# A first inverse product on 64 rows of TensorE per l, summed over c, in place of one on 128 rows

## The chip, the cores and the metric

One Trainium2 chip, one of its cores. The metric is the device time of one execution in microseconds; the time shown for a kernel is the median of several runs. TensorE is called PE in the profile, VectorE DVE, ScalarE ACT, GpSimd POOL, and SyncE, which issues most transfers, SP.

## What is computed

A Fourier filter along the sequence, then two expert layers on the 24576 rows that come out of it:

```python
X = np.fft.rfft(x, axis=1)                       # x: (8, 3072, 256)
Yr = Xr @ w_r - Xi @ w_i + b_r
Yi = Xr @ w_i + Xi @ w_r + b_i
Yr = np.sign(Yr) * np.maximum(np.abs(Yr) - 0.01, 0.0)
Yi = np.sign(Yi) * np.maximum(np.abs(Yi) - 0.01, 0.0)
x  = np.fft.irfft(Yr + 1j * Yi, n=3072, axis=1).reshape(-1, 256)
h  = np.maximum(x @ w_in, 0.0)                   # w_in: (256, 2048)
x  = h * h @ w_out                               # w_out: (2048, 256)
...
```

What follows (a soft mixture of 8 experts with 4 slots each) is not touched by the change.

## The kernel before

The transform of length 3072 is two products with small matrices, 96 x 32, and so is its inverse. The first part of the kernel works on 96 units, 12 for each of the 8 sequences. A unit holds two of 24 frequency groups; l (0 or 1) says which of the two, and c (0 or 1) the real or the imaginary part. A unit u goes through these steps, in the loop over half steps h (U = h // 2) at the end of the listing:

- `a_mm`, `a_out`: the product with the 96-point matrix, on PE (tile psA), copied out by ACT and written to DRAM (ad). It runs ahead of the units, at two thirds of a step per half step.
- `load_b`, `b_mm`: the values of two units come back from DRAM (bt), and the product with the 32-point matrix bm gives psB.
- `b_hi`, `b_lo`, `b_sum`: psB is split into a high and a low part (Xh, Xl), and a third operand, real plus imaginary, is formed (Sf, Sh, Sl).
- `l_mm`: the linear layer, as three products of split operands: psL and psS. psL's 128 rows are (l, k), 64 rows for each l; its columns are (c, d).
- `l_move`: DVE adds the bias to psS (st), and adds st to psL. It does so in four pieces of 64 rows by 256 columns, since the result ub has rows (c, k) and columns (l, d): each piece goes to another half of the rows.
- `l_relu`, `l_soft`: the soft threshold, on ACT (ua) and DVE (ub).
- `c_mm`, `c_out`: the first inverse product. PE takes for each l the 128 rows (c, k) of ub against cm, two matmuls of 256 columns into one bank (psC); ACT copies the bank (sc), and SP writes it to DRAM (zd) in four transfers.

All eight PSUM banks belong to one pool (psP, tag "g"), of which psA, psB, psL, psS and psC take a bank each in turn. The order on each engine is the order of the calls; nothing else schedules. In the even half step of U come `b_mm(U)`, `l_mm(U-2)`, `l_soft(U-4)`, `b_lo(U-1)`, `c_out(U-5)`, the first stage and `l_relu(U-3)`; in the odd one `c_mm(U-4)`, `l_move(U-2)`, `b_hi(U)`, `b_sum(U-1)`, the first stage and, for every second U, `load_b(U+3)`. Beside it `decode` unpacks the weights of the expert layer (operations from line 374 on, on DVE, ACT and POOL). In the last units the second inverse product of the first sequence is made (`stage_d`, psY, yf, yl). The second part of the kernel, the expert layers, begins with the first matmul into psA of line 633.

```python
            nc.tensor.matmul(p[:, l], lhsT=cm[:, 2 * (u % NU) + l], rhs=ub[:, l], start=True, stop=True)
```

is the matmul of the first inverse product, in `c_mm`.

Of the kernel before, what the change touches and what calls it, by code (L numbers as in the profile page):

```python
# [10 lines left out]
F32 = mybir.dt.float32  # L11
# [4 lines left out]
ALU = mybir.AluOpType  # L16
AX = mybir.AxisListType
PSUM = bass.MemoryType.PSUM
# [5 lines left out]
N2 = 32  # L24
NP = 24
DM = 256
# [7 lines left out]
def shape_constants():  # L34

    n1 = np.arange(N1)
    n2 = np.arange(N2)
    k = np.arange(48)
    ang = 2 * np.pi * np.outer(n1, k) / N1
    f1 = np.zeros((N1, N1))
    f1[:, :48] = np.cos(ang)
    f1[:, 48] = np.cos(np.pi * n1)
    f1[:, 49:] = -np.sin(ang[:, 1:])
    bm = np.zeros((2, 2, N2, NP, 2, 2, N2))
    cm = np.zeros((2, 2, N2, NP, 2, 2, N2))  # L50
    for p in range(NP):
        for h in range(2):
            k1 = p + NP * h
            for k2 in range(N2):
                if k1 == 0 and k2 == 0:
                    bm[0, h, :, p, 0, h, 0] = 1.0
                    bm[0, h, :, p, 1, h, 0] = (-1.0) ** n2
                    cm[0, h, 0, p, 0, h, :] = 1.0
                    cm[1, h, 0, p, 0, h, :] = (-1.0) ** n2
                elif k1 == 0:  # L60
                    kk, cin = (96 * k2, 0) if k2 < 16 else (48 + 96 * (k2 - 16), 1)
                    ph = 2 * np.pi * ((n2 * kk) % SEQ) / SEQ
                    bm[cin, h, :, p, 0, h, k2] = np.cos(ph)
                    bm[cin, h, :, p, 1, h, k2] = -np.sin(ph)
                    cm[0, h, k2, p, cin, h, :] = 2 * np.cos(ph)
                    cm[1, h, k2, p, cin, h, :] = -2 * np.sin(ph)
                else:
                    kk = k1 + 96 * k2
                    s = 1.0 if k2 < 16 else -1.0
                    ph = 2 * np.pi * ((n2 * kk) % SEQ) / SEQ  # L70
                    bm[0, h, :, p, 0, h, k2] = np.cos(ph)
                    bm[1, h, :, p, 0, h, k2] = np.sin(ph)
                    bm[0, h, :, p, 1, h, k2] = -s * np.sin(ph)
                    bm[1, h, :, p, 1, h, k2] = s * np.cos(ph)
                    cm[0, h, k2, p, 0, h, :] = np.cos(ph)
                    cm[1, h, k2, p, 0, h, :] = -s * np.sin(ph)
                    cm[0, h, k2, p, 1, h, :] = np.sin(ph)
                    cm[1, h, k2, p, 1, h, :] = s * np.cos(ph)

    order = np.array([NC * t + c for c in range(NC) for t in range(TB)])  # L80
    cm = cm[..., order]
    dm = np.zeros((N1, 104))
    dm[0, :N1] = 1.0 / SEQ
    dm[48, :N1] = np.cos(np.pi * n1) / SEQ
    dm[1:48, :N1] = 2 * np.cos(ang[:, 1:]).T / SEQ
    dm[49:, :N1] = -2 * np.sin(ang[:, 1:]).T / SEQ
    j = np.arange(128)
    cst = np.zeros((128, 4, 128))
    cst[:, 0] = np.eye(128)
    same = (j[:, None] % 32) == (j[None, :] % 32)  # L90
    cst[:, 1] = same
    for g in range(2):
        cst[:, 2 + g] = same & ((j[:, None] % 32) // 4 == 4 * g + j[:, None] // 32)
    f = np.float32
    return {
        "c_f1": f1.astype(f),
        "c_bm": np.ascontiguousarray(bm.reshape(128, NP, 128).astype(f)),
        "c_cm": np.ascontiguousarray(cm.reshape(128, NP, 128).astype(f)),
        "c_dm": dm.astype(f),
        "c_st": cst.astype(f),  # L100
    }
# [3 lines left out]
def fft_moe_kernel(ctx, tc, x, w_r, w_i, b_r, b_i, moe_w_in, moe_w_out, moe2_phi, moe2_w1, moe2_w2,  # L105
                   c_f1, c_bm, c_cm, c_dm, c_st, out):
    nc = tc.nc
# [4 lines left out]
    NU = NP // 2  # L112
# [56 lines left out]
    cm = k1p.tile([128, NP, 128], F32, tag="cm", name="cm")  # L169
# [13 lines left out]
    wkb = wka = psP = None  # L183
    xt, xs, pa, bt, pb, xb, sp, pl, sh, pc, ad = {}, {}, {}, {}, {}, {}, {}, {}, {}, {}, {}
    cur = {}

    def pbank(name):
        return psP.tile([128, 512], F32, tag="g", name=name)
# [109 lines left out]
            mm3(s, h[:, dh], l[:, dh], lwh[0][:, dh], lwl[0][:, dh], dh == 0, dh == 1)  # L298
        pl[u] = (p, s)

    def l_move(u):

        p, q = pl.pop(u)
        ub = wkb.tile([128, 2, DM], F32, tag="ub", name=f"ub{u}", bufs=3)
        st = wkb.tile([128, 2, DM], F32, tag="st", name=f"st{u}", bufs=1)
        nc.vector.tensor_tensor(out=st, in0=q.unsqueeze(1).broadcast_to([128, 2, DM]), in1=bias[u % NU == 0],
                                op=ALU.add)
        for l in range(2):
            s = slice(64 * l, 64 * l + 64)
            for c in range(2):  # L310
                nc.vector.tensor_tensor(out=ub[64 * c:64 * c + 64, l], in0=p[s, c], in1=st[s, c], op=ALU.add)  # L311
        sh[u] = [ub]

    def l_relu(u):
# [6 lines left out]
        nc.vector.scalar_tensor_tensor(out=ub, in0=ub, scalar=LAM, in1=ua, op0=ALU.add, op1=ALU.min)  # L321

    def c_mm(u):
        ub = sh.pop(u)[0]
        p = pbank(f"psC{u}").rearrange("p (l d) -> p l d", l=2)
        for l in range(2):
            nc.tensor.matmul(p[:, l], lhsT=cm[:, 2 * (u % NU) + l], rhs=ub[:, l], start=True, stop=True)  # L327
        pc[u] = p

    def c_out(u):  # L330
        b, k = divmod(u, NU)
        t = wkb.tile([128, 2, DM], F32, tag="sc", name=f"sc{u}")
        nc.scalar.copy(t, pc.pop(u))
        z = zd[b].rearrange("r c t d -> r (c t) d")
        for ch in range(4):
            r = NP * ch + 2 * k
            nc.sync.dma_start(out=z[r:r + 2].rearrange("q n d -> n q d"), in_=t[N2 * ch:N2 * ch + N2])


    wide = moe_w_in.dtype != F32  # L340
# [125 lines left out]
    XB, XL = 4, NB * NC  # L466
    with tc.manual_schedule():
        psp = ExitStack()
        psP = psp.enter_context(tc.tile_pool(name="psP", bufs=8, space=PSUM))
        wkbx, wkax = ExitStack(), ExitStack()  # L470
        wkb = wkbx.enter_context(tc.tile_pool(name="wkb", bufs=2, side="right", reuse_waits="tile"))
        wka = wkax.enter_context(tc.tile_pool(name="wka", bufs=2, side="right", reuse_waits="tile"))
# [17 lines left out]
            load_x(c)  # L490
        nc.sync.dma_start(bm[:, :4], c_bm[:, :4])
        wr, wi, wn = (wkb.tile([128, 2, DM], F32, tag="ub", name=s, bufs=3) for s in ("wr", "wi", "wn"))
        wm = wkb.tile([128, 2, DM], F32, tag="sc", name="wm")

        def copy(j):
            return nc.scalar.copy if j % 2 else nc.vector.tensor_copy
# [37 lines left out]
        def at(u, *steps):  # L534
            if 0 <= u < NT:
                for g in steps:
                    g(u)

        for h in range(2 * NT + 12):
            U, o = divmod(h, 2)  # L540

            j = -1
            if (h < 8 or (h + 1) * 2 // 3 > h * 2 // 3) and aj < NB * NA + 1:
                j, aj = aj, aj + 1
            def first_stage():
                if NA <= j < NB * NA:
                    a_mm(j)
                    if j % 2:
                        load_x(j // 2 + XB)
                if j >= NA + 1:  # L550
                    a_out(j - 1, nc.scalar.copy)

            if o == 0:
                at(U, b_mm)
                at(U - 2, l_mm)
                at(U - 4, l_soft)
                at(U - 1, b_lo)
                at(U - 5, c_out)
                first_stage()
                at(U - 3, l_relu)  # L560
            else:
                at(U - 4, c_mm)
                at(U - 2, l_move)
                at(U, b_hi)
                at(U - 1, lambda u: b_sum(u, nc.gpsimd))
                first_stage()
                if U % 2 and U + 3 < NT:
                    load_b(U + 3)

            if h % 4 == 2 and h < 18:  # L570
                nc.sync.dma_start(bm[:, h + 6:h + 10], c_bm[:, h + 6:h + 10])
            if h % 4 == 1 and h < 24:
                nc.sync.dma_start(cm[:, h - 1:h + 3], c_cm[:, h - 1:h + 3])
            if h == 14:
                nc.sync.dma_start(ident, c_st[:, 0])
                nc.sync.dma_start(dmt, c_dm)
                nc.sync.dma_start(phi, moe2_phi.rearrange("(a p) n -> p a n", p=128))
                nc.vector.memset(acc, 0.0)
                nc.vector.memset(ss, 0.0)
                nc.vector.memset(nm[0], 3.0e38)  # L580
            if h == 16:
                weight_tiles()
            if h > 16:
                for _ in range(1 + (h % 6 == 0)):
                    next(dec_run, None)
            if U == NT - YL and o == 1:
                drain(dec_run)
                wkax.close()
                yp[0] = ypx.enter_context(tc.tile_pool(name="yp0", bufs=1, reuse_waits="tile"))
                load_z(0)  # L590
                ylead = stage_d(0, pbank)
            if ylead is not None and U > NT - YL + 1:
                next(ylead, None)
# [246 lines left out]
        nM, cw, st = (rt.tile([128, 1], F32, tag=t, name=t) for t in ("nM", "cw", "st"))  # L840
# [7 lines left out]
        for n in range(NSB * NW + 1):  # L848
            s, q = divmod(n, NW)
# [110 lines left out]
        p = bank_o("01", "p_m2")  # L960
# [173 lines left out]
```

## Time and profile before

| | us |
|---|---|
| median of 3 runs | 2882.76 |
| lowest and highest of them | 2878.36, 2883.17 |
| the profiled execution: its time | 2878.61 |
| the profiled execution: its span | 2876.8 |
| of the span: PE busy | 2806.6 (98%) |
| of the span: DVE busy | 2149.8 (75%) |
| of the span: ACT busy | 1685.9 (59%) |

The span runs from the first instruction to the last. PE's busy time is made of starts that were recorded and ends that are modelled, so matmuls that follow each other closely overlap in it: where the rows give a time from one start to the next, that is what a matmul costs in a stream. A matmul of float32 leaves two records, two passes over the same columns; one of float32r (the products of split operands) leaves one. The first part of the kernel, which holds the change, is the first 534 us.

### The profile page before, as it was taken

The page shows a single profiled execution, that of the slowest core. Times are in us where ns is not written, and L with a number is a line of the kernel's source. Part 1 is how long each engine was busy: PE and PEld are TensorE (multiplying, and loading weights), DVE is VectorE, ACT ScalarE, POOL GpSimd, SP SyncE. Part 2 cuts the span into 40 slices and gives each one's busy share as a digit, 9 for nine tenths or more (in the row PEclk, how much of TensorE's full clock was granted, in tenths as well). Part 3 has the DMA queues.
Part 4 walks back from the last instruction along what each step waited for, and adds up shares of the span by engine and source line. Part 5 has one row for each costly group of instructions (what it writes and reads, how often), then busy time and mean ns, then how long its engine had stood idle before and what let it go on. Part 6 is the DMA issues. An engine that isn't in the chain of part 4 may idle for free.

```text
span 2876.8 us, 46778 instructions
## 1 busy us (share of the span) xinstructions
PE 2806.6 (98%) x17543; PEld 2639.8 (92%) x17543; DVE 2149.8 (75%) x4458; ACT 1685.9 (59%) x3720; POOL 174.2 (6%) x236
## 2 busy tenths in 40 slices
PE   8999999899999999999999999999999999999995
PEld 5788889899999999999999999999999999999974
DVE  4899999777777777777777777777777777777764
ACT  3677775565555656565656565656565656565543
POOL 0344541000000000000000000000000000000000
PEclk9999999999999999999999999999999999999997
DMA  9888885200000000000000000000000000000169
GB/s 270 230 231 228 237 219 144 61 12 12 15 12 15 12 15 12 15 12 15 12 15 12 15 12 20 12 15 12 18 14 15 12 15 12 15 12 4 37 234 367
DMA packets 106389, 190.07 MB, mean 66 GB/s; under 512 B 14930, under 2 KB 75730, under 8 KB 103218
## 3 DMA queue, kind: packets, MB, share of 16 engines
q1 hardware_dynamic: 102946, 180.78, 21.9%
q10 hardware_dynamic: 3216, 6.29, 0.6%
q8 instruction: 138, 2.26, 0.3%
q14 instruction: 89, 0.73, 0.1%
HBM read 108.38 MB, written 78.64 MB: 65 GB/s over the span
## 4 chain that ended last, share of the span: by engine, by line
PE 90%; DVE 5%; DMA 3%; ACT 1%; issue 1%; SPq 1%; POOL 0%; DVEq 0%; ACTq 0%; POOLq 0%
PE psA L633 19%; PE psX L633 14%; PE psO L119 12%; PE psO L120 12%; PE psO L118 12%; PE psY L433 4%; PE psA L208 3%; PE psC L327 2%; PE psB L243 2%; PE px L714 1%; DVE ub L311 1%; PE psL L118 1%; PE psL L119 1%; PE psL L120 1%; DMA out_dram<-ob 1%; PE pz L730 1%
## 5 line engine op out<-in xcount | busy, mean ns | idle before, releaser
L119 PE MATMUL psO<-gl,wo 128*128 128x384 f32 x2048 | 687.4, 336 | 0.0
L120 PE MATMUL psO<-gh,wo 128*128 128x384 f32 x2048 | 684.7, 334 | 0.0
L118 PE MATMUL psO<-gh,wo 128*128 128x384 f32 x2048 | 684.6, 334 | 0.0
L673 DVE TENSOR_TENSOR gl<-g,gh 128x384 fp32r<-128x384 f32 x1024 | 557.1, 552 | 91.1 <-ACT gh L656 75.4
L119 PEld LDWEIGHTS psO<-gl,wo 128*128 128x128 f32 x2048 | 384.4, 188 | 7.3 <-DVE gl L673 7.3
L120 PEld LDWEIGHTS psO<-gh,wo 128*128 128x128 f32 x2048 | 384.5, 188 | 0.0
L118 PEld LDWEIGHTS psO<-gh,wo 128*128 128x128 f32 x2048 | 384.5, 188 | 0.0
L633 PE MATMUL psA<-yh,wia 128*128 128x384 f32 x1024 | 353.2, 345 | 12.6 <-ACT r L649 12.1
L633 PE MATMUL psA<-yh,wib 128*128 128x384 f32 x1024 | 348.1, 340 | 0.9 <-ACT V L639 0.8
L633 PE MATMUL psX<-yh,wia 128*128 128x384 f32 x1024 | 343.1, 335 | 0.0
L644 DVE TENSOR_TENSOR h<-psX,r 128x384 f32<-128x384 f32 x256 | 142.7, 557 | 249.5 <-PE psX L633 247.7
L649 ACT ACTIVATE r<-psA 128x384 f32<-128x384 f32 x256 | 126.1, 492 | 303.3 <-PE psA L633 262.4
L665 DVE SCALAR_TENSOR_TENSOR g<-h 128x384 f32<-128x384 f32 x512 | 281.8, 550 | 0.1
L639 ACT COPY r<-psA 128x384 f32<-128x384 f32 x256 | 123.3, 482 | 262.9 <-PE psA L633 262.9
L644 DVE TENSOR_TENSOR h<-psX,W 128x384 f32<-128x384 f32 x256 | 142.8, 558 | 178.5 <-ACT W L639 177.6
L656 ACT CAST gh<-g 128x384 fp32r<-128x384 f32 x512 | 263.0, 514 | 14.7 <-DVE g L665 11.9
L667 DVE TENSOR_TENSOR g<-r 128x384 f32<-128x384 f32 x512 | 260.3, 550 | 0.1
L639 ACT COPY W<-psA 128x384 f32<-128x384 f32 x256 | 123.3, 482 | 222.3 <-PE psA L633 220.7
L658 ACT ACTIVATE gh<-r 128x384 fp32r<-128x384 f32 x512 | 240.7, 518 | 8.1
L633 PEld LDWEIGHTS psA<-yh,wia 128*128 128x128 f32 x1024 | 192.7, 188 | 27.9 <-ACT r L649 16.9
L644 DVE TENSOR_TENSOR h<-psX,V 128x384 f32<-128x384 f32 x256 | 141.7, 554 | 76.0 <-PE psX L633 68.6
L633 PEld LDWEIGHTS psA<-yh,wib 128*128 128x128 f32 x1024 | 192.4, 188 | 2.1 <-ACT V L639 1.7
(214 smaller groups left out, 5339.6 us busy)
## 6 DMA issues: line engine op xcount, KB each, us to landing
bt<-ad SPq DMA_DIRECT2D x192, 128.0 KB, 4.5
zd<-sc SPq DMA_DIRECT2D x384, 64.0 KB, 2.8
zt<-zd SPq DMA_DIRECT2D x64, 384.0 KB, 3.5
xt<-in_x_dram SPq DMA_DIRECT2D x63, 384.0 KB, 4.3
ad<-sa SPq DMA_DIRECT2D x56, 384.0 KB, 4.2
out_dram<-ob SPq DMA_DIRECT2D x21, 1024.0 KB, 18.3
w<-in_moe_w_dram SPq DMA_DIRECT2D x5, 1024.0 KB, 12.3
raw<-in_moe_w_in_dram SPq DMA_DIRECT2D x16, 256.0 KB, 3.8
```

The source lines that it names most:

```text
L118: nc.tensor.matmul(o, lhsT=ah, rhs=bh, start=start, stop=False)
L119: nc.tensor.matmul(o, lhsT=ah, rhs=bl, start=False, stop=False)
L120: nc.tensor.matmul(o, lhsT=al, rhs=bh, start=False, stop=stop)
L633: nc.tensor.matmul(p, lhsT=w[:, k, l], rhs=r[:, j], start=start and n == 0, stop=n == 2, skip_group_check=True)
L639: nc.scalar.copy(t, self.a)
L644: nc.vector.tensor_tensor(out=h, in0=self.x, in1=t, op=ALU.add)
L649: nc.scalar.activation(out=t, in_=self.g[k].pop() if k in self.g else self.a, func=AF.Relu)
L656: nc.scalar.copy(h, self.g[k][0])
L658: nc.scalar.activation(out=h, in_=self.g[k][0], func=AF.Square)
L665: nc.vector.scalar_tensor_tensor(out=g, in0=t, scalar=0.0, in1=t, op0=ALU.max, op1=ALU.mult)
L667: nc.vector.tensor_tensor(out=g, in0=t, in1=t, op=ALU.mult)
L673: nc.vector.tensor_tensor(out=l, in0=g, in1=f(h), op=ALU.subtract)
```

## The change

In `c_mm` the product is made for each l on that l's own 64 rows, (k) alone, and the two parts c are summed in PSUM by two matmuls, the first with `start`, the second with `stop`. The matmuls of l = 0 read rows 0 to 63 of ub and cm, those of l = 1 rows 64 to 127, and l = 0 and l = 1 write different banks. So ub stays in psL's layout, rows (l, k) and columns (c, d), and DVE's four moves become one addition (`l_add`). Two units share the two banks: the even unit takes the first half of the columns of each, the odd one the second. `c_out` copies both banks after the odd unit, and writes two units with four transfers. The pool psP gives 6 banks to tag "g" and 2 to tag "c". The constant cm is laid out anew to fit, sc is one buffer for two units where it was two buffers for one, and a start-up tile (wm) moves from sc's place to that of ua.

```diff
-        "c_cm": np.ascontiguousarray(cm.reshape(128, NP, 128).astype(f)),
+        "c_cm": np.ascontiguousarray(cm.reshape(2, 64, NP // 2, 2, 128).transpose(3, 1, 2, 0, 4).reshape(128, NP, 128)
+                                     .astype(f)),
...
-    def l_move(u):
+    def l_add(u):
...
-        for l in range(2):
-            s = slice(64 * l, 64 * l + 64)
-            for c in range(2):
-                nc.vector.tensor_tensor(out=ub[64 * c:64 * c + 64, l], in0=p[s, c], in1=st[s, c], op=ALU.add)
+        nc.vector.tensor_tensor(out=ub, in0=p, in1=st, op=ALU.add)
...
     def c_mm(u):
         ub = sh.pop(u)[0]
-        p = pbank(f"psC{u}").rearrange("p (l d) -> p l d", l=2)
-        for l in range(2):
-            nc.tensor.matmul(p[:, l], lhsT=cm[:, 2 * (u % NU) + l], rhs=ub[:, l], start=True, stop=True)
-        pc[u] = p
+        if u % 2 == 0:
+            pc[0] = [psP.tile([128, 2, DM], F32, tag="c", name=f"psC{u}_{l}", bufs=2) for l in range(2)]
+        for c in range(2):
+            for l in range(2):
+                s = slice(64 * l, 64 * l + 64)
+                nc.tensor.matmul(pc[0][l][:, u % 2], lhsT=cm[s, 2 * (u % NU) + c], rhs=ub[s, c], start=c == 0, stop=c == 1)
 
     def c_out(u):
-        b, k = divmod(u, NU)
-        t = wkb.tile([128, 2, DM], F32, tag="sc", name=f"sc{u}")
-        nc.scalar.copy(t, pc.pop(u))
+        if u % 2 == 0:
+            return
+        b, k = divmod(u - 1, NU)
+        t = wkb.tile([128, 2, 2, DM], F32, tag="sc", name=f"sc{u}", bufs=1)
+        for l in range(2):
+            nc.scalar.copy(t[:, :, l], pc[0][l])
+        t = t.rearrange("p u l d -> p (u l) d")
...
-            nc.sync.dma_start(out=z[r:r + 2].rearrange("q n d -> n q d"), in_=t[N2 * ch:N2 * ch + N2])
+            nc.sync.dma_start(out=z[r:r + 4].rearrange("q n d -> n q d"), in_=t[N2 * ch:N2 * ch + N2])
...
-        psP = psp.enter_context(tc.tile_pool(name="psP", bufs=8, space=PSUM))
+        psP = psp.enter_context(tc.tile_pool(name="psP", bufs=6, space=PSUM))
```

On PE, in the middle of the first part (the number behind a tile's letters is the unit's), the first inverse product of unit 56 stood between the linear layer of unit 58 and the next product of the first stage:

```order
L119 MATMUL psS58_4676<-lwl0_90,Sh58_4642 128x256
L120 MATMUL psS58_4676<-lwh0_87,Sl58_4643 128x256
L327 MATMUL psC56_4699<-ub56_4558,cm_86 128x256 x2
L208 MATMUL psA103_4717<-xt51_4267,f1t_84 96x512
L243 MATMUL psB61_4726<-bm_85,bt60_4494 128x2x64 x4
```

Now it stands at the same place, as four matmuls that go to two banks by turns:

```order
L120 MATMUL psS58_4473<-lwl0_90,Sh58_4439 128x256
L121 MATMUL psS58_4473<-lwh0_87,Sl58_4440 128x256
L329 MATMUL psC56_0_4497<-ub56_4366,cm_86 128x256
L329 MATMUL psC56_1_4498<-ub56_4366,cm_86 128x256
L329 MATMUL psC56_0_4497<-ub56_4366,cm_86 128x256
L329 MATMUL psC56_1_4498<-ub56_4366,cm_86 128x256
L209 MATMUL psA103_4515<-xt51_4086,f1t_84 96x512
L244 MATMUL psB61_4524<-bm_85,bt60_4298 128x2x64 x4
```

So every unit has, in one place, matmuls on 64 rows between matmuls on 96 or 128 rows; nothing else on PE has moved.

On ACT, a few units earlier, each unit had its copy of psC (unit 53, then unit 54) between others:

```order
L333 COPY sc53_4540<-psC53_4470 128x512
L219 COPY sa98_4492<-psA99_4488 96x512
L316 ACTIVATE ua55_4550<-ub55_4473,nlam_95 128x512
...
L123 CAST Sh57_4569<-Sf57_4537 128x256
L333 COPY sc54_4605<-psC54_4555 128x512
L219 COPY sa100_4615<-psA100_4546 96x512
L316 ACTIVATE ua56_4617<-ub56_4558,nlam_95 128x512
```

Now two copies stand behind the odd unit, and none behind the even one:

```order
L337 COPY sc53_4344<-psC52_0_4216 128x2x256
L337 COPY sc53_4344<-psC52_1_4217 128x2x256
L220 COPY sa98_4296<-psA99_4292 96x512
L314 ACTIVATE ua55_4355<-ub55_4280,nlam_95 128x512
...
L124 CAST Sh57_4374<-Sf57_4341 128x256
L220 COPY sa100_4414<-psA100_4351 96x512
L314 ACTIVATE ua56_4416<-ub56_4366,nlam_95 128x512
```

The copies of units 52 and 53 stand together, in the place of unit 53's.

## Rows read from the trace of the kernel before

**Rows 1.** The page: busy time of each engine over the span.

```profile
PE 2806.6 (98%) x17543; PEld 2639.8 (92%) x17543; DVE 2149.8 (75%) x4458; ACT 1685.9 (59%) x3720; POOL 174.2 (6%) x236
```

**Rows 2.** Windows: stretch, length, busy us (x records) of PE PEld DVE ACT POOL, clock, DMA, GB/s.

```profile
0.00:96.00 96.00, 80.31 (x386) 55.13 (x387) 48.47 (x102) 38.22 (x78) 9.01 (x15) 0.97 0.93 263
96.00:216.00 120.00, 118.95 (x770) 99.34 (x769) 113.55 (x246) 84.27 (x196) 53.03 (x73) 1.00 0.86 228
216.00:336.00 120.00, 119.79 (x784) 100.22 (x783) 113.56 (x245) 83.81 (x195) 55.24 (x73) 1.00 0.87 232
336.00:481.00 145.00, 145.00 (x995) 126.29 (x995) 133.34 (x287) 97.07 (x217) 49.50 (x66) 1.00 0.75 201
481.00:534.00 53.00, 44.47 (x316) 40.37 (x314) 50.63 (x103) 27.26 (x59) 7.40 (x10) 1.00 0.38 90
```

**Rows 3.** Chain of waits, 153 to 453 us: start, us, what.

```profile
153.33 0.86 PE psC L327 x4
154.20 0.86 PE psA L208 x2
155.06 0.89 PE psB L243 x8
...
159.77 0.89 PE psB L243 x8
...
449.46 0.89 PE psB L243 x8
...
453.31 0.89 PE psB L243 x8
```

**Rows 4.** Chain of waits, 480 to 540 us.

```profile
491.60 0.70 DVE ub L321
...
528.89 0.70 DVE ub L321
...
532.09 0.70 DVE ub L321
...
534.32 2.08 PE psC L327 x4
```

**Rows 5.** Chain of waits, 60 to 100 us.

```profile
72.88 4.96 DMA cm<-in_c_cm_dram
...
84.89 4.81 DMA raw<-in_moe_w_in_dram
```

**Rows 6.** Groups by line, 0 to 560 us: xcount | busy us, mean ns | idle before.

```profile
L311 DVE TENSOR_TENSOR ub<-psL,st 64x256 f32<-64x256 f32 x384 | 162.0, 422 | 7.1
L260 DVE TENSOR_TENSOR Xl<-psB,Xh 128x512 fp32r<-128x512 f32 x96 | 66.4, 691 | 3.1
L333 ACT COPY sc<-psC 128x512 f32<-128x512 f32 x96 | 56.3, 586 | 15.8 <-PE psC L327 15.0 <-DMA bt<-ad 0.3 <-DMA zd<-sc 0.3
```

**Rows 7.** Timeline at 2817.5 us: matmuls on 32 rows each, four row groups.

```profile
2817.33 0.76 PE L1093 MATMUL pf<-ro,cc 32*128 32x256 f32 x8
```

**Rows 8.** The tile pf: engine, count, duration ns min/median/max, first and last start.

```profile
L1093 PE MATMUL pf<-ro,cc x384: 374/375/792, 2810.8 to 2851.4; 32*128 32x256 f32 x192
```

**Rows 9.** Timeline of PE at 2739.5 us: start, us; 64*128 is 64 rows.

```profile
2739.69 0.33 PE L119 MATMUL psO<-gl,wo 128*128 128x384 f32 x1
2739.86 0.34 PE L120 MATMUL psO<-gh,wo 128*128 128x384 f32 x1
2740.13 0.40 PE L724 MATMUL py<-ident,lg 64*128 64x64 f32 x3
2740.37 0.35 PE L724 MATMUL py<-ident,e 64*128 64x64 f32 x3
2740.65 0.45 PE L633 MATMUL psA<-yh,wia 128*128 128x384 f32 x1
```

**Rows 10.** Timeline of PE at 1528 us, from 32 columns back to 128.

```profile
1527.72 0.83 PE L706 MATMUL pl<-xm,phi 128*32 128x384 f32 x8
1528.48 0.44 PE L633 MATMUL psA<-yh,wia 128*128 128x384 f32 x1
```

**Rows 11.** Windows, psC alone: stretch, length, busy us (x records) PE PEld ACT, clock, DMA, GB/s.

```profile
96.00:216.00 120.00, 25.20 (x96) 17.60 (x95) 13.41 (x23) 1.00 0.86 228
216.00:336.00 120.00, 23.86 (x92) 16.69 (x92) 14.08 (x24) 1.00 0.87 232
336.00:481.00 145.00, 30.98 (x120) 21.44 (x120) 17.17 (x30) 1.00 0.75 201
```

**Rows 12.** Waits of PE and its weight loads, 96 to 481 us: total, times, longest.

```profile
PEld psC L327 <- DVE Sf L261: 2.1, 8, 0.3
PEld psC L327 <- DVE ub L321: 2.1, 4, 1.1
...
PE psC L327 <- DVE ub L321: 1.3, 3, 0.8
PEld psC L327 <- DVE Xl L260: 1.1, 4, 0.3
```

More of the change, by code (lines that the diff above doesn't have):

```diff
@@ L324, in c_mm, with c_out @@
         ub = sh.pop(u)[0]
-        p = pbank(f"psC{u}").rearrange("p (l d) -> p l d", l=2)
-        for l in range(2):
-            nc.tensor.matmul(p[:, l], lhsT=cm[:, 2 * (u % NU) + l], rhs=ub[:, l], start=True, stop=True)
-        pc[u] = p
-    def c_out(u):
-        b, k = divmod(u, NU)
-        t = wkb.tile([128, 2, DM], F32, tag="sc", name=f"sc{u}")
-        nc.scalar.copy(t, pc.pop(u))
+        if u % 2 == 0:
[4 more added lines that the diff above has]
+                nc.tensor.matmul(pc[0][l][:, u % 2], lhsT=cm[s, 2 * (u % NU) + c], rhs=ub[s, c], start=c == 0, stop=c == 1)
+    def c_out(u):
+        if u % 2 == 0:
+            return
+        b, k = divmod(u - 1, NU)
+        t = wkb.tile([128, 2, 2, DM], F32, tag="sc", name=f"sc{u}", bufs=1)
+        for l in range(2):
+            nc.scalar.copy(t[:, :, l], pc[0][l])
+        t = t.rearrange("p u l d -> p (u l) d")
         z = zd[b].rearrange("r c t d -> r (c t) d")
@@ L492, in fft_moe_kernel @@
         wr, wi, wn = (wkb.tile([128, 2, DM], F32, tag="ub", name=s, bufs=3) for s in ("wr", "wi", "wn"))
-        wm = wkb.tile([128, 2, DM], F32, tag="sc", name="wm")
+        wm = wkb.tile([128, 2, DM], F32, tag="ua", name="wm", bufs=1)
         def copy(j):
@@ L562, in fft_moe_kernel @@
                 at(U - 4, c_mm)
-                at(U - 2, l_move)
+                at(U - 2, l_add)
                 at(U, b_hi)
```

## The prediction

> **What bounds the kernel now.** I read first the busy times of the span, then windows by stage, then the chain of waits in the stage that the change touches, then the groups of instructions, and last the few places where PE already does what the change asks of it.
>
> PE is busy 98% of the span and DVE 75% [rows 1]. An average says little, so the windows: from 96 to 481 us PE is busy 118.95 of 120, 119.79 of 120 and 145.00 of 145 us, DVE 113.55, 113.56 and 133.34 [rows 2]. Both look full. Which of them sets the pace is told by the chain: there it consists of PE's matmuls without a gap, psC 0.86, psA 0.86, psB 0.89 us, and two units are 159.77 - 155.06 = 4.71 us apart [rows 3]. **PE is the bound of this stage**; DVE is just fast enough. Late in it, where psA has run out, a unit takes PE 453.31 - 449.46 = 3.85 us [rows 3].
>
> From 481 to 534 us it is the other way round: DVE is busy 50.63 of 53 us, PE 44.47 [rows 2], and the chain runs from one soft threshold to the next, eight of them in 528.89 - 491.60 = 37.29 us, 4.66 each [rows 4]. **DVE is the bound there.** The first 96 us wait for transfers: PE is busy 80.31, and the chain has two waits of nearly 5 us for DMA, cm and raw [rows 2, 5].
>
> **The change part by part.**
>
> *DVE.* Four additions of 64x256, 422 ns each, go: 1.69 us a unit. One of 128x512 comes; its nearest row is the subtraction from psB in the same shape, also PSUM with SBUF, 691 ns [rows 6]. So 1.0 us less for every unit.
>
> *PE, the matmuls themselves.* Before: four records of 256 columns in 0.86 us, 0.215 each [rows 3]. After: eight, each of 256 columns, on half the rows. Whether the halves run beside each other is shown where the output is made: there matmuls of 32 rows and 256 columns float32 go to four row groups and four banks, and eight records take 0.76 us from the first start to the last end [rows 7]; one after the other they would need 7 x 0.215 = 1.5 us before the last began, and one lasts 0.37 [rows 8]. So row groups do overlap. Two groups then make four steps of 0.215 out of eight records: 0.86 again, **nothing gained or lost**. The other extreme, no overlap, is eight steps, 1.72 us.
>
> *PE, going into the tile of 64 rows and out.* The kernel has this form once: six small matmuls on 64 rows between two on 128 [rows 9]. In a stream the psO matmuls start 0.17 us apart and last 0.34, so one starts 0.17 before its predecessor's modelled end (2739.69 and 2739.86). The first on 64 rows starts at 2740.13, only 0.07 before the end at 2740.20. PE's pipeline ran empty for 0.10 more. On the way back it is the same: the six end at 2740.37 + 0.35 = 2740.72, psA starts at 2740.65, 0.07 before. The way back from 32 columns gives 0.07 as well (1527.72 + 0.83 = 1528.55 against 1528.48) [rows 10]. So 0.10 each way. And the first matmul after a switch has its weights' load in front of it, which elsewhere lies under the matmul before: psA takes 0.45 us there instead of psO's 0.34 for the same 128x384, 0.11 more [rows 9]; going in, the first three take 0.40 and the next three 0.35, 0.05 more [rows 9]. I take 0.10 going in, since psC's weights are 128 columns wide like psA's. **Sum: 0.10 + 0.10 + 0.10 + 0.11 = 0.41 us a unit.** Bounds: 0.20 if both loads stay hidden, 0.65 if each way costs the whole overlap of 0.17 and each load 0.15.
>
> From 96 to 481 us psC has 96 + 92 + 120 = 308 records [rows 11], four to a unit: 77 units. PE is the bound, so 77 x 0.41 = **+31.6 us**. (Bounds +15.4 and +50.)
>
> *DVE's stalls of PE in that stage.* They go, since DVE gets 1.0 us of slack and PE is slower. PE is idle 1.05 + 0.21 + 0 us in the windows [rows 2]; the rows that name DVE before psC add up to 2.1 + 2.1 + 1.3 + 1.1 = 6.6 [rows 12], partly under matmuls still running. I take **-2** (bounds 0 and -6.6).
>
> *The last stage.* DVE needs 4.66 - 1.0 = 3.66 us a unit, PE 3.85 + 0.41 = 4.26. PE becomes the bound, 0.40 less than 4.66, for the 46 us from 483 to 529, ten units: -4.0. Behind them lies one more l_move before the last thresholds (529 to 532 us) [rows 4], -1.0; the last psC, 2.08 us [rows 4], is followed by psA and pays its own switch, some +0.4. Together **-4.6**.
>
> *The first 96 us.* Some six units' psC lie there. Their 2.5 us is put under the wait for raw, which ends when it lands; I take 0 (bounds 0 and +2.5).
>
> *ACT, SP and the banks.* ACT has the same two copies of 586 ns for two units [rows 6], and is busy 84 of 120 us [rows 2]. SP issues half as many writes for the same bytes. A pair of units now waits for both copies of the pair before it, since each bank of psC has no second buffer. But the copies stand one half step ahead, and between psC of the odd unit and the next pair's psC lie psB, twelve psL and six psS, about 4.71 - 0.86 - 0.86 = 3 us [rows 3], against 1.17 us of copies; I cost it at nothing. If ACT's queue were half a microsecond late, it would be paid once in two units, 38 x 0.5 = 19 us. With six banks psL and psS take banks that DVE freed in the unit before; DVE now frees them earlier than it did. Nothing.
>
> Sum: 31.6 - 2 - 4.6 + 0 = **+25 us**, on the profiled execution's 2878.61: 2903.6. The median of the runs lies 4.15 above that execution, so 2907 to 2908; I say 2907. Of a difference from no change about 0.2%, 5.8 us, can be told here.
>
> **The rivals.**
>
> *1. The switch is free, and only DVE's saving is left (faster).* Were the weights loaded and the pipeline kept full across the change of tile, PE would stay at its pace, DVE's stalls (-2) would go, and in the last stage the bound would fall from 4.66 to PE's 3.85, -8, and the tail -1: 2882.8 - 11 = 2872. It decides at a price of 0.08 us a unit, where 77 units cost the 6 us that the end gives back. For it: the rows show one switch to 64 rows, with small transposes. Against: three switches, two kinds of tile, the same 0.10 [rows 9, 10]. Chance 0.08.
>
> By the Trainium skill (TensorEngine Tiling (Array Packing), Key Properties) a change of tiling mode drains the engine; it gives no size, and by it alone this rival would have no chance. The 0.10 each way agrees.
>
> *2. The row groups do not run beside each other here.* Eight steps in place of four, 0.86 more for each of 77 units, +66: 2973. Against: [rows 7], though with 32 rows and without sums in a bank. Chance 0.05.
>
> *3. The second pass of a float32 matmul holds up the other row group.* If the two passes of l = 0 must start before the first of l = 1, the steps form a staircase: five instead of four, 0.215 x 77 = +17: 2924. Against: eight records in such a staircase need at least four steps, 3 x 0.215 + 0.37 = 1.02 us, and took 0.76 [rows 7]. Chance 0.04.
>
> The Trainium skill (TensorE: Matmul & The Clock Gate, Part 3, what overlaps and what doesn't) says that matmuls are strictly first in, first out, without reordering, which taken for passes gives this rival; the 0.76 us disagrees.
>
> *4. The banks.* The pair's wait of the last part, +19: 2926. Chance 0.03.
>
> **How the numbers follow.** Forecast 0.80, rivals as above. The forecast's own range: price 0.20 to 0.65 a unit, +15.4 - 9 = +6 to +50 - 5 = +45, most of it between 2889 and 2927; rivals 3 and 4 end within it. Rivals 1 and 2, 0.13 together, and some of the forecast's ends stay outside: 2888 to 2928. Faster by over 0.2%: rival 1 and a little, 0.09. The same: a price near 0.1, 0.05. Slower: the rest, 0.86.
>
> **What would show it.** In the profile after: eight psC records a unit that take about 1.07 us on the chain where four took 0.86, and a load of weights in the open behind them, before psA or psB, so that two units are 5.1 us apart where they were 4.71; DVE's group of 128x512 additions at about 690 ns x96, and DVE busy some 85 of 120 us where it was 113; in the last units psB 4.26 us apart, on PE; the first psA of line 633 near 560 instead of 536 us. I am wrong if psC's eight records are stretched over 1.5 us or more (rival 2), if psA or psB starts 0.215 behind the last psC (rival 1), or if PE waits for ACT's copy sc before an even unit's psC (rival 4).

## The result and the profile after

| | before | after |
|---|---|---|
| median, us | 2881.76 (four runs) | 2903.11 (four runs) |
| lowest and highest, us | 2878.36, 2883.17 | 2900.64, 2908.02 |
| profiled execution: time, span | 2878.61, 2876.8 | 2900.64, 2898.8 |

The ratio of after to before is 1.0078, interval 1.006 to 1.0095: **21 us slower**. The prediction said 2907, between 2888 and 2928. The profiled executions differ by 22.03 us; where these lie is told from them.

The page of after, busy time by engine ([rows 1]):

```profile
PE 2836.1 (98%) x17927; PEld 2632.5 (91%) x17927; DVE 2039.9 (70%) x4170; ACT 1691.3 (58%) x3720; POOL 177.5 (6%) x236
```

DVE has lost 110 us of work, PE has gained 30, and the time went with PE. By stage, the windows of after (the columns of [rows 2]):

```profile
96.00:216.00 120.00, 120.00 (x822) 91.91 (x822) 82.03 (x165) 82.36 (x187) 51.60 (x69) 1.00 0.81 222
216.00:336.00 120.00, 120.00 (x822) 92.06 (x820) 80.81 (x163) 80.97 (x182) 54.26 (x72) 1.00 0.77 213
336.00:481.00 145.00, 145.00 (x1003) 111.87 (x1000) 95.59 (x189) 93.74 (x208) 52.53 (x67) 1.00 0.75 203
481.00:534.00 53.00, 53.00 (x432) 47.39 (x433) 37.67 (x72) 31.08 (x66) 8.07 (x12) 1.00 0.44 118
```

From 96 to 534 us PE is never idle. DVE went from 113.55 to 82.03 of 120 us and waits: in the groups by line of after (0 to 580 us; line, engine, operation, count, busy us, mean ns, idle before and its cause; [rows 6]) the operation ahead of the addition, st, waits 141.3 us for psS, where it waited 14.3 us in before (last line, 0 to 560 us).

```profile
L309 DVE TENSOR_TENSOR ub<-psL,st 128x512 f32<-128x512 f32 x96 | 66.4, 691 | 3.3
L307 DVE TENSOR_TENSOR st<-psS,bias 128x512 f32<-128x512 f32 x96 | 66.3, 691 | 146.7 <-PE psS L121 141.3 <-DMA bias<-in_b_r_dram 5.4
```

```profile
L306 DVE TENSOR_TENSOR st<-psS,bias 128x512 f32<-128x512 f32 x96 | 65.7, 684 | 20.2 <-PE psS L120 14.3 <-DMA bias<-in_b_r_dram 5.6
```

The addition takes 691 ns x96, as the subtraction of the same shape did before. On PE, the chain of waits of after in the long stage ([rows 3]):

```profile
161.06 1.06 PE psC L329 x8
162.13 1.09 PE psB L244 x8
...
166.21 1.06 PE psC L329 x8
167.28 1.03 PE psA L209 x2
```

psC's eight records take 1.06 us where four took 0.86: +0.20. Whatever follows psC is longer too: psA 1.03 where it took 0.86, psB 1.09 where it took 0.89. Two units are 166.21 - 161.06 = 5.15 us apart. Call a stretch of matmuls on 64 rows, between matmuls on 96 or 128 rows, a visit to the 64-row tile. So **a visit to the 64-row tile costs 0.37 or 0.40 us**. The timeline of after shows it at one switch (start, us, engine, line, tile):

```profile
546.37 0.28 PE L120 MATMUL psS<-lwl,Sh 128*128 128x256 f32 x1
...
546.49 0.28 PE L121 MATMUL psS<-lwh,Sl 128*128 128x256 f32 x1
546.70 0.73 PEld L329 LDWEIGHTS psC<-ub,cm 64*128 64x128 f32 x8
546.70 1.14 PE L329 MATMUL psC<-ub,cm 64*128 64x256 f32 x8
...
547.76 0.19 PEld L119 LDWEIGHTS psL<-lwh,Xh 128*128 128x128 f32 x1 [0.33 <-issue]
547.76 0.39 PE L119 MATMUL psL<-lwh,Xh 128*128 128x256 f32 x1
...
547.99 0.28 PE L120 MATMUL psL<-lwl,Xh 128*128 128x256 f32 x1
```

The psS matmuls start 0.12 apart; psC starts 0.21 behind the last of them, 0.09 more. The loads of psC and psL begin together with their matmuls, not under the matmul before, and psL's first matmul takes 0.39 where the next takes 0.28.

In the last units ([rows 4]) the chain, which was DVE's, is PE's, with psC 4.23 us apart; then it goes to ACT and to transfers of sc:

```profile
505.28 1.06 PE psC L329 x8
...
509.51 1.06 PE psC L329 x8
...
543.38 1.06 PE psC L329 x8
...
546.77 1.06 PE psC L329 x8
...
550.15 1.11 PE psC L329 x8
...
553.65 2.29 DMA zd<-sc
...
558.45 2.40 DMA zd<-sc
...
...
562.02 1.33 PE psA L638 x3
```

**Where the 22.03 us lie**, from the starts of the same matmuls in both traces (each unit's first psL; the expert layers' first psA and first psO), beside the forecast's terms:

| from | to | the end's time in before | shift there in after | of it in this stretch | forecast |
|---|---|---|---|---|---|
| start | unit 9 | 98.1 | -0.7 | -0.7 | 0 |
| unit 9 | unit 86 (77 units) | 485.2 | +26.2 | +26.8 | +31.6 - 2 |
| unit 86 | first psA | 535.8 | +19.0 | -7.2 | -4.6 |
| first psA | first psO | 543.3 | +22.7 | +3.8 | 0 |
| first psO | end | 2876.8 | +22.0 | -0.7 | 0 |

### The profile page after: what moved, and what is told of

It reads as the page before. It is cut to its first block, busy times and chain, and to the rows that moved or that the text cites. A ratio compares the mean times of both kernels' runs of the same rounds, so it can differ in the third digit from the quotient of the medians.

```text
span 2898.8 us, 46941 instructions
## 1 busy us (share of the span) xinstructions
PE 2836.1 (98%) x17927; PEld 2632.5 (91%) x17927; DVE 2039.9 (70%) x4170; ACT 1691.3 (58%) x3720; POOL 177.5 (6%) x236
## 4 chain that ended last, share of the span: by engine, by line
PE 93%; DMA 3%; DVE 2%; SPq 1%; ACT 1%; issue 0%; POOL 0%; DVEq 0%; ACTq 0%
PE psA L638 18%; PE psX L638 14%; PE psO L120 12%; PE psO L121 12%; PE psO L119 12%; PE psY L438 4%; PE psA L209 4%; PE psC L329 3%; PE psB L244 3%; PE psL L119 2%; PE psL L120 2%; PE psL L121 2%; PE px L719 1%; DMA out_dram<-ob 1%; PE pz L735 1%; PE pl L711 1%
```

## The experiments

Theory A: PE bounds the first part, and the change pays a fixed price for each visit to the 64-row tile; the rest is the wait for the single sc buffer at the end. The rivals are named with each run.

### The addition alone

```diff
-        for l in range(2):
-            s = slice(64 * l, 64 * l + 64)
-            for c in range(2):
-                nc.vector.tensor_tensor(out=ub[64 * c:64 * c + 64, l], in0=p[s, c], in1=st[s, c], op=ALU.add)
+        nc.vector.tensor_tensor(out=ub, in0=p, in1=st, op=ALU.add)
```

This is the kernel before with that edit only; it leaves out the change on PE, so its product mixes l and c and is not the reference's.

> The kernel before, with DVE's part of the change alone: one addition of 128x512 in place of the four moves. ub is then left in the linear layer's rows while PE's two matmuls on 128 rows stay as they were, so the first inverse product mixes l and c. PE's work is that of the kernel before, to the instruction. Theory A (PE bounds the long stage; DVE's relief is worth its few stalls there and the last units): the stalls of about 3 us, the last units from 4.66 to 3.85 us each, about 8, and the tail 2 go: 13 us faster than before, about 2869. Theory B (DVE and PE bound the stage together, so 1.0 us a unit counts in full): 77 us faster, about 2805. If PE's steady pace is 4.71 and 5.57 us between units as before, A holds.

Measured: 2867.81, ratio to before 0.9951 (0.9938 to 0.9965), 14.3 us faster. Its chain in the long stage and in the last units:

```profile
159.28 0.86 PE psC L324 x4
...
163.98 0.86 PE psC L324 x4
...
168.74 0.86 PE psC L324 x4
...
502.48 0.86 PE psC L324 x4
...
506.33 0.86 PE psC L324 x4
```

163.98 - 159.28 = 4.70 and 168.74 - 163.98 = 4.76: the long stage keeps its pace with DVE relieved of 1 us a unit, so PE bounds it; the last units go from DVE's 4.66 to PE's 3.85. By the starts of the same matmuls, as in the table above, the 77 units of the long stage take 2.3 us less than in before, and the stretch from unit 86 to the first psA 10.8 less. That is what DVE's part of the change is worth when nothing is paid for it on PE.

### Half as many visits, and c = 0 and c = 1 apart

The first joins the matmuls of an even and an odd unit. The other two make c = 1 a visit of its own, behind the next unit's linear layer or ahead of it.

```diff
         if u % 2 == 0:
-            pc[0] = [psP.tile([128, 2, DM], F32, tag="c", name=f"psC{u}_{l}", bufs=2) for l in range(2)]
+            return
+        pc[0] = [psP.tile([128, 2, DM], F32, tag="c", name=f"psC{u}_{l}", bufs=2) for l in range(2)]
+        for v in (u - 1, u):
+            ub = sh.pop(v)[0]
...
```

> The changed kernel, with the matmuls on 64 rows of two units behind each other, after the odd unit: half as many visits to the tile of 64 rows, the same matmuls. Theory A (the loss is the way into the tile of 64 rows and back, about 0.38 us a visit): 38 visits fewer in the stage that PE bounds and some in the last units, 15 to 18 us less than the changed kernel, about 2887, still slower than before; two units 10.2 us apart become 9.85. Theory B (the eight matmuls themselves are slower on half the rows, or six banks hold PE up): the time of the changed kernel, 2903, or a little more, since DVE's addition now waits for a longer stretch of PE.

```diff
+    def c_half(u, c):
+        ub = sh[u][0]
+        for l in range(2):
+            s = slice(64 * l, 64 * l + 64)
+            nc.tensor.matmul(pc[0][l][:, u % 2], lhsT=cm[s, 2 * (u % NU) + c], rhs=ub[s, c], start=c == 0, stop=c == 1)
...
-                at(U - 5, c_out)
+                at(U - 5, lambda u: c_half(u, 1), c_out)
```

> The changed kernel, with each unit's four matmuls on 64 rows in two places: c = 0 where they stand, c = 1 in the half step after, behind the linear layer. Twice as many visits to the tile of 64 rows, the same matmuls. Theory A (the loss is about 0.38 us a visit): 77 visits more in the stage that PE bounds and 11 in the last units, 29 to 34 us more than the changed kernel, about 2935. Theory B (the matmuls themselves are slower, or the banks hold PE up): the time of the changed kernel, 2903, within 3 us.

```diff
                 at(U, b_mm)
+                at(U - 5, lambda u: c_half(u, 1))
                 at(U - 2, l_mm)
```

> The changed kernel, with c = 1 of each unit's matmuls on 64 rows moved to the next half step, behind psB and ahead of the linear layer: every unit goes into the tile of 64 rows twice, and ACT's copy sc, which held PE up where c = 1 stood behind the linear layer, has the linear layer's 2 us to itself again. Theory A (0.36 to 0.39 us a visit): 96 visits more, of which some 89 in stretches that PE bounds, 32 to 35 us more than the changed kernel, about 2937; each four records on 64 rows then take 0.32 + 0.215 us of PE, and psC in the chain two pieces a unit. Theory B (a visit costs more when it is short, as the 56 us of the run before suggests, 0.6 a visit): 2955 or more, without PE waiting for sc.

| | median, us | ratio to before | against after, us |
|---|---|---|---|
| two units joined | 2883.91 | 1.0007 (0.9998 to 1.0016) | -19.2 |
| c = 1 behind the linear layer | 2958.95 | 1.0268 (1.0254 to 1.0283) | +55.8 |
| c = 1 ahead of it | 2933.2 | 1.0185 (1.0171 to 1.0199) | +30.1 |

Chain of two units joined, then of c = 1 ahead of the linear layer:

```profile
162.40 0.86 PE psA L209 x2
163.26 1.93 PE psC L331 x16
165.19 1.03 PE psA L209 x2
```

```profile
159.36 0.63 PE psC L331 x4
160.00 1.03 PE psA L209 x2
```

One visit with 4, 8 or 16 records takes 0.63, 1.06 and 1.93 us. At two records to 0.215 us these would be 0.43, 0.86 and 1.72: each time 0.20 or 0.21 more, and psA behind it 0.17 more. **The price belongs to the visit and not to its length**, and both doubling and halving the visits moved the time accordingly, by 30.1 us for a forecast of 32 to 35 and by 19.2 for 15 to 18. The traces show it without the scatter of the runs: from unit 9 to unit 86 (77 units) the shift against before is +13.2 us with a visit for two units, +26.8 with one for each (after), +55.2 with two (c = 1 ahead of the linear layer). That is 13.7 us for 38.5 visits and 28.4 for 77, 0.36 and 0.37 each.

The middle run missed its 2935 by 24 us, and it tells little of the price. Its waits from 150 to 430 us (engine, line, waited for, us in total, times, longest) have two that the others lack:

```profile
PEld psC L331 <- ACT sc L341: 22.7, 32, 1.1
...
PE psC L331 <- ACT sc L341: 5.3, 8, 0.7
```

With c = 1 so late, ACT's copies came too late for the next pair's banks. That is the wait of rival 4, brought about by the experiment; besides, where no psA stands between c = 1 of one unit and c = 0 of the next, two visits run into one. The run ahead of the linear layer has neither.

### The buffer of sc

The last two pairs of units write sc into buffers of bt, which is no longer used there.

```diff
-        t = wkb.tile([128, 2, 2, DM], F32, tag="sc", name=f"sc{u}", bufs=1)
+        if u < NT - 3:
+            t = wkb.tile([128, 2, 2, DM], F32, tag="sc", name=f"sc{u}", bufs=1)
+        else:
+            t = wkb.tile([128, 4, DM], F32, tag="bt", name=f"sc{u}").rearrange("p (u l) d -> p u l d", u=2)
```

> The changed kernel, with the last two pairs of units copied into buffers of their own (bt's, which nothing loads any more) in place of the single sc. Theory A (at the end of the first part ACT waits for the write of the pair before, and the expert layer's first copies queue behind it): the waits of ACT before sc, some 5 us in the trace of the changed kernel, go, and the expert layer's first steps run as closely as before: 4 to 5 us less than the changed kernel, about 2899. Theory B (the expert layer waits there for something else anyway): no difference, 2903.

Measured: 2898.0, ratio 1.0058 (1.0045 to 1.0071), 5.1 less than after. The two intervals overlap, so the size is better taken from the traces: from the first psA to the first psO it takes 4.2 us less, and the same edit on top of the joined units, below, takes the same 4.2 us off that stretch (11.27 to 7.05). What it removes is seen in the timeline of after (in brackets: idle before, and what ended it):

```profile
556.04 1.07 ACT L337 COPY sc<-psC 128x512 f32<-128x512 f32 x2 [3.08 <-DMA zd<-sc]
557.00 0.50 ACT L644 COPY r<-psA 128x384 f32<-128x384 f32 x1
...
557.55 0.45 PE L638 MATMUL psA<-yh,wib 128*128 128x384 f32 x1 [1.43 <-ACT r L644]
...
561.07 0.51 ACT L661 CAST gh<-g 128x384 fp32r<-128x384 f32 x1 [2.15 <-DMA zd<-sc]
...
562.02 0.69 PE L638 MATMUL psA<-yh,wia 128*128 128x384 f32 x1 [1.88 <-ACT W L644]
```

and in the same part of the chain of this run:

```profile
556.31 1.05 ACT sc L340 x2
557.36 0.39 ACT r L647
...
557.79 0.80 PE psA L641 x3
```

In after the last pair's copies wait 3.08 us until the pair before has been written from the one buffer. The expert layers' copy r stands behind them in ACT's queue, and PE waits 1.43 us for it. Then ACT waits once more, 2.15 us, for a write of sc, ahead of gh and the copy W; the first psA at the slow pace follows W, after 1.88 us without work on PE. With the buffer apart both waits are gone.

The wait is paid a second time by PE's clock, which falls behind it. The windows of after, and of this run, at the entry to the expert layers (the last three columns: granted clock, DMA share, GB/s):

```profile
555.00:558.00 3.00, 1.57 (x8) 1.25 (x8) 0.47 (x1) 1.46 (x3) 0.00 (x0) 1.00 0.15 39
558.00:562.00 4.00, 2.10 (x8) 1.16 (x7) 1.03 (x3) 1.37 (x3) 0.00 (x0) 0.65 0.93 237
562.00:566.00 4.00, 3.98 (x12) 3.66 (x13) 2.23 (x5) 1.53 (x4) 0.00 (x0) 0.50 0.35 106
```

```profile
558.00:562.00 4.00, 3.40 (x16) 2.21 (x15) 2.58 (x6) 1.97 (x5) 0.00 (x0) 1.00 0.90 215
562.00:566.00 4.00, 4.00 (x22) 3.82 (x23) 3.44 (x7) 3.15 (x7) 0.00 (x0) 1.00 0.51 129
```

In after PE was busy 1.57 of 3 and 2.10 of 4 us, and from 562 to 566 its granted clock is 0.50, the lower level of 1.2 GHz; three psA behind a wait take 1.33 us there, and 0.80 at the full clock in this run. From the first psA to the first psO it takes 11.25 us, in this run 7.05, before 7.49. Of the 4.2 us between the two, 1.4 lie behind the wait for W, where PE works without a pause (562.02 to 566.06 us in after, 560.57 to 563.23 in this run): that is the clock's part, and the other 2.8 lie before it, in the stretch with the waits.

### Both repairs together

Two units joined, and the last two pairs' sc in bt's buffers.

> The changed kernel with both edits of the first call: two units behind each other on 64 rows, and buffers of their own for the last two pairs of sc. Theory A (the two are independent): 2884 less 5, about 2879, within 0.2% of the kernel before. Theory B (the wait for sc was part of what the pairing gave back): 2884.

Measured: 2880.13, ratio 0.9997 (0.9988 to 1.0006): no different from before. The 48 visits that are left cost some 13 us (0.9 us less than before here, 14.3 less with the addition alone), about what DVE's part gives.

### How the eight half-row records run

The loops over c and l are exchanged:

```diff
-        for c in range(2):
-            for l in range(2):
+        for l in range(2):
+            for c in range(2):
```

> The changed kernel, with the loops over l and c of the matmuls on 64 rows exchanged: both matmuls of l = 0, then both of l = 1. Nothing else differs. Theory A (a matmul runs beside the one before it if its rows are free, and matmuls start in the program's order): l = 1 starts only when the second matmul of l = 0 has started, six steps of 0.215 us in place of four, 0.43 us a unit more, 33 us in the long stage and 5 in the last units, about 2941. Theory B (the order does not matter, PE picks what has its rows free): four steps, 2903. Theory C (the two halves do not run beside each other at all in either kernel): the same in both, 2903, and no two starts within 10 ns.

and the same four matmuls are made on all 128 rows:

```diff
-                s = slice(64 * l, 64 * l + 64)
-                nc.tensor.matmul(pc[0][l][:, u % 2], lhsT=cm[s, 2 * (u % NU) + c], rhs=ub[s, c], start=c == 0, stop=c == 1)
+                nc.tensor.matmul(pc[0][l][:, u % 2], lhsT=cm[:, 2 * (u % NU) + c], rhs=ub[:, c], start=c == 0, stop=c == 1)
```

> The changed kernel, with its four matmuls a unit on all 128 rows of ub[:, c] and cm in place of 64: no tile of 64 rows, and nothing beside each other. The sums over c then mix the two l. DVE's part, banks, copies and writes are those of the changed kernel. Theory A (in the changed kernel the halves share their time and a visit costs 0.38): eight steps of 0.215, 0.86 us a unit over the kernel before and no visit, 66 us in the long stage, less 3 of stalls, and 2 to 3 for the end: about 2947. Theory B (the loss of the changed kernel comes from six banks, the shared pair and the copies, not from PE's tile): the same loss comes on top, 2965 or more, and PE waits for ACT or DVE in the rows.

Measured: loops exchanged 2902.82, ratio 1.0078 (1.0064 to 1.0092), the time of after; on 128 rows 2945.4, ratio 1.0225 (1.0211 to 1.0239), +42.3 against after. Chains of the two:

```profile
160.79 1.07 PE psC L329 x8
```

```profile
164.12 1.73 PE psC L328 x8
165.85 0.86 PE psA L209 x2
```

Eight records on 128 rows take 1.73 us, eight steps of 0.215, and the psA behind them 0.86: no visit, no price. DVE's part, the banks, the copies and the writes are those of after in this run, and from unit 9 to unit 86 it loses 63.2 us to before: 77 x 0.86 = 66 less the 2.3 of DVE's part. So the six banks and the shared pair cost nothing in the long stage. On half the rows they take 1.06 with the price's 0.20 in it, so the two row groups do run beside each other, sums in a bank included. The starts of the eight records of one unit (us from the first, from the records of the traces):

```
after             0  0.007  0.320  0.327  0.536  0.542  0.752  0.758
loops exchanged   0  0.013  0.320  0.333  0.536  0.549  0.752  0.765
```

In both they start in pairs, 0.216 apart but for the first step, where a load is in the open. Records on the same rows start at least 0.215 apart (the 1.73 us), so a pair is taken to be one record of each l, though with the loops exchanged both matmuls of l = 0 stand first in the program. The records do not name their rows, but their semaphores agree, in both kernels. In an even unit, which begins a new pair of banks, the weight loads of the first two records both wait for ACT, which empties the two banks in two copies. In an odd unit, behind which ACT copies, the two matmul records that signal completion, one for each bank, are the last pair. So with the loops exchanged, too, the second matmul of l = 0 ends beside the second of l = 1, and theory B holds: four steps in either order.

### The change where DVE bounds

The kernel before, with the change for the last sequence alone, in which DVE was the bound: its twelve units take the new cm (loaded over the old one), the one addition, and a bank for each l. In the second run they are also joined by two, and the last two pairs write sc from bt's buffers.

```diff
+        if u >= NT - NU:
+            nc.vector.tensor_tensor(out=ub, in0=p, in1=st, op=ALU.add)
...
+        if u >= NT - NU:
+            pc[u] = [pbank(f"psC{u}_{l}")[:, :DM] for l in range(2)]
+            for c in range(2):
+                for l in range(2):
+                    s = slice(64 * l, 64 * l + 64)
+                    nc.tensor.matmul(pc[u][l], lhsT=cm[s, 2 * (u % NU) + c], rhs=ub[s, c], start=c == 0, stop=c == 1)
+            return
```

> The kernel before for seven of the eight sequences; the change (one addition on DVE, four matmuls on 64 rows, with a bank for each l and unit) for the twelve units of the last one alone, whose cm is loaded anew into its place when the seventh sequence has used it. There DVE is the bound, and PE has some 0.8 us a unit to spare for a visit to the tile of 64 rows. Theory A (the change gains where DVE is the bound and loses where PE is): ten units at 4.25 in place of 4.66 us, -4, and a tail shorter by about 2.5 as in the changed kernel's trace: 6 to 7 us faster than before, about 2875. Theory B (the reload of cm or the banks take it back): no difference from before.

> As the run before it in this call, with two units of the last sequence behind each other on 64 rows, and the last two pairs copied into bt's buffers. Theory A (a visit costs 0.36 to 0.39 us): six visits fewer where PE is then the bound, 2 us less than the run before it, about 2873, 9 us faster than before. Theory B (DVE's own pace, 3.66 us a unit, or the wait of its addition for the longer stretch of PE sets the end): no gain over the run before it.

Measured: 2873.5, ratio to before 0.9975 (0.9965 to 0.9986), 6.9 us faster; joined 2868.66, ratio 0.9965 (0.9952 to 0.9977), 11.7 us faster. Among the kernels that make the whole computation this is the fastest, ahead of both. Its chain:

```profile
500.43 1.93 PE psC L339 x16
...
508.60 1.93 PE psC L339 x16
```

8.17 us for two units, 4.09 each, against 4.23 with a visit for each and 4.66 before. Over six pairs that is 1.7 of the 4.8 us between the two medians. The traces of the two runs differ by 3.6 us, and 2.4 of these lie before unit 9, where the two kernels are still alike: that part is scatter between executions. From unit 86 to the first psA the traces show 7.2 us less than before in the first run and 8.9 in the second, which is the 1.7 again.

## Why the prediction was right, and where not

**The bound: right.** PE bounds the stage from 96 to 481 us; with DVE relieved alone, 77 units took 2.3 us less, the stalls for which -2 was forecast.

**PE, the matmuls themselves: right.** Four steps for eight records, 0.86 again. Rivals 2 and 3 fall: eight steps take 1.73 and not 1.06, and neither order of the loops gives a fifth step. The Trainium skill (TensorE: Matmul & The Clock Gate, Part 3, what overlaps and what doesn't) says that matmuls are strictly first in, first out. Between row groups the starts in pairs with the loops exchanged do not agree with that.

**PE, going into the tile and out: right in its mechanism, a little too dear.** 0.37 to 0.40 instead of 0.41: by the starts in the records 0.09 each way of empty pipeline, 0.10 for psC's first load in the open, 0.007 for the second record of the last pair, and for the load behind it 0.07 before psA and 0.10 before psB. I had taken 0.11 for both. Rival 1 falls. With DVE's stalls of -2, the long stage was forecast at +29.6 and came to +26.8; with the 2.3 of the addition alone that is 29.1 us for 77 visits, 0.38 each. Rival 1's limit of 0.08 was too low by the forecast's own terms: 77 units at 0.08 cost 6 of the 11 us that the end and the stalls give back, so 11 / 87 = 0.13 a visit decides, and by the run with the addition alone 14.3 / 96 = 0.15.

**The last stage: -4.6 forecast, -7.2 measured.** The pace was right, 4.23 for 4.26. The tail was mis-sized: the last psC, 2.08 us [rows 4], was taken for what four records cost there. It was twice the usual because the clock was low, which I had not looked up: in the run with the addition alone the same four records take 1.15 us there, at a granted clock of 1.00. The windows of before:

```profile
530.00:533.00 3.00, 0.99 (x5) 0.54 (x4) 2.68 (x6) 1.10 (x3) 0.00 (x0) 1.00 0.18 40
533.00:536.00 3.00, 2.77 (x9) 1.93 (x9) 0.69 (x1) 1.13 (x2) 0.00 (x0) 0.62 0.32 72
```

PE had been busy 0.99 of 3 us while DVE finished, and the granted clock was 0.62 in the next 3, below its level of 2.4 GHz. After the change the clock stays at 1.00 until 558 us, and the same piece takes 1.14 us. That gives 0.9 where I had added 0.4. Of the other 1.3, the last two units give 1.2. No psB stands there any more, so PE needs 3.39 us from psC to psC (543.38, 546.77 and 550.15 in the chain of after) and not 4.26. From psL to psL the two took 8.67 us before and 6.71 after, 1.96 less, where the forecast had 0.8.

**ACT, SP and the banks: the step that failed.** "I cost it at nothing" weighed the copies against the banks in the steady stage, and there nothing was paid. I did not ask what the single buffer of sc does where pairs come close together, at the end, where two copies queue ahead of the expert layers' own. It cost 3.8 us against before; with the buffer apart 4.2 came back in the traces, 1.4 of them the clock's. Rival 4 was the wrong wait at the wrong place.

So the sum of 25 came to 22.0 on the profiled executions: -2.8 in the long stage, -2.6 in the last, +3.8 at the entry, and -0.7 each in the first 96 us and after the entry. That the sum came out within 3 us is in part luck, since the misses have both signs; the range, 40 us wide, would have held them even with one sign, 10.6 us together. The term that was called nothing was the largest of them.

## What to carry to other kernels

Before work is taken off an engine, ask in each stage whether that engine sets the pace, and make the change only where it does: here DVE's relief on all 96 units cost 21 us, and on the last 12 it gave 7 to 12. Here matmuls on 64 of TensorE's rows cost a fixed price for each visit between matmuls on 96 or 128, so gather them into few visits. A buffer that suffices in the steady stage must be looked at again where the stage ends and another kind of work queues behind its wait; and a matmul's duration is read with the granted clock beside it.

## What was not expected of the hardware

- Two matmuls of different row groups start within 7 to 13 ns of each other, also when the second stands behind another matmul of the first group in the program (shown by the spacing of the records and by their semaphores).
- A visit to the 64-row tile costs 0.20 us within and 0.17 to 0.20 behind it, the same for 4, 8 and 16 records.
- Two waits on ACT, of 3.08 and 2.15 us, left PE busy 1.57 of 3 and 2.10 of 4 us; the next 4 us of PE ran at a granted clock of 0.50, in which three psA took 1.33 us instead of 0.80.
